# A searched instruction order, a last output tile in three pieces, and one weight's loads moved to the GpSimd queue

## The chip, the cores and the metric

One core of a Trainium2 chip. The metric is the device time of one execution in microseconds. The profile's span starts and ends a little inside the timed execution (266.0 us for a timed 267.67), so differences are taken within one kind of number only.

## The reference, cut to what matters

A gated mix of two branches over x of 2048 x 512: attention in four segments of 512 rows with 32 heads of 16 and a memory carried from segment to segment, and a gated linear unit of width 1792.

```python
g = sigmoid((x * gate_w).sum(-1, keepdims=True))
# attention: q, k, v = x@wq, x@wk, x@wv; per segment softmax(q k' + mask) v,
#   mixed with phi(q) M / (phi(q) z); then M += phi(k)' v, z += sum phi(k); o @ wo
# unit: h = relu(x @ W_gate) * (x @ W_up); h @ W_down
return g * a + (1 - g) * b
```

## The kernel before

The kernel is written as about a thousand small operations with names, engines, planned durations and keys. A planner, run when the kernel is built, orders them per engine, and that order is what is emitted. An array mode is the way in which TensorE's array is divided for a matmul: whole ("D"), row strips ("R"), strips of 64 x 32 ("P") or column strips ("C"). `f12.3` is the score block 3 of segment 1, head group 2; `pv12` its product with V; `mz0`, `den1` memory product and denominators; `g`, `u`, `d` the dense products of the unit, `q`, `k`, `v`, `wo` those of the attention, in operations of two matmuls.

```python
# the planner: TensorE takes the ready operation with the least key; a change of array mode is penalised
k = o.key
if o.mode == "P":            # product with V, 64 x 32 strips
    k += -20.0 if mode == "R" else 4.0
elif o.mode == "D" and mode == "C" and "C" not in o.flex:
    k += 3.0
...
o.ran = mode if mode in o.flex else o.mode   # dense work may stay in column strips ("C")

def mm(out_ap, lhsT, rhs, start, stop):
    if tiling[0] == "C":
        for j in range(4):                   # four column strips, four small matmuls
            q = slice(32 * j, 32 * j + 32)
            nc.tensor.matmul(out_ap[q], lhsT=lhsT[:, q], rhs=rhs, start=start, stop=stop, tile_position=(0, 32 * j))
    else:
        nc.tensor.matmul(out_ap, lhsT=lhsT, rhs=rhs, start=start, stop=stop)
...
def c_dummy(e):                              # "warm-up" matmuls on constants while x is loaded
    for _ in range(31):
        nc.tensor.matmul(g_dummy.t[:, 0:P], lhsT=ones, rhs=ones, start=True, stop=True)
...
x0_part(0, 0, "SP", -300)
x0_part(0, 1, "ACT", -300)
wq_part(0, 1, "ACT", -299)
x0_part(1, 0, "SP", -299)
x0_part(1, 1, "POOL", -110)
wq_part(1, 2, "SP", -298)
wq_part(2, 3, "POOL", -80)
wq_part(3, 4, "POOL", -79)
...
# wk's load waits for a one-element write into wk_sb, which waits for the first copied piece of x
o_wk0 = op("wk0", {"DVE": 0.08}, lambda e: nc.vector.memset(wk_sb[0:1, 0, 0:1], 0.0), key=-600, cls=0)
lw["wk"].deps.append((o_wk0, None))
```

## Time and profile before

| before | value |
|---|---|
| time, median of 3 runs | 267.61 us (267.2 to 268.28) |
| span of the profiled run | 265.97 us |
| busy: TensorE, ScalarE, VectorE, GpSimd | 98, 74, 68, 66% |
| first wk matmul to start of the last matmul | 10.23 to 262.30 us |
| instruction packets of queue 8, taken for TensorE's (why: under the load of x) | 21 of 16 KB |

TensorE is nearly always busy, so the table's third and fourth rows are the ones to read: the time is a head (before the first wk matmul), a stretch of TensorE work, and a tail. The lines that carry this are in the prediction.

### The profile page before, as it was taken

The numbers are of one execution on the slowest core, as the hardware profiler recorded it, in microseconds if no ns is written. First come the engines' busy times: TensorE is split into PE (matmuls) and PEld (weight loads), VectorE is DVE, ScalarE is ACT, GpSimd is POOL, SyncE is SP. The second block draws the span as 40 slices with busy tenths as digits, with TensorE's granted clock in tenths as the row PEclk, the third lists the DMA queues.
The fourth block names the chain that finished last, engine by engine and source line by source line (L and its number), as shares of the span: only waits on it lengthen the run. The fifth ranks groups of instructions, "written<-read, shape, count | busy, mean of one in ns | idle before, by whom it ended". The sixth has DMA issues, their size and how long they took to land.

```text
span 266.0 us, 6927 instructions
## 1 busy us (share of the span) xinstructions
PE 261.4 (98%) x2760; PEld 115.1 (43%) x2760; DVE 181.3 (68%) x408; ACT 195.7 (74%) x191; POOL 175.7 (66%) x436
## 2 busy tenths in 40 slices
PE   8999999999999999999999999999999999999994
PEld 7443344444344444444344434344434444344453
DVE  1496878998877188887988726678986625566611
ACT  3598899898976658999986668898788665876020
POOL 8338788884567678884567978886758876537000
PEclk9999999999999999999999999999999999999999
DMA  6898932224650100000582010000030010000011
GB/s 161 268 275 183 328 88 81 83 79 102 157 115 22 41 22 2 0 2 20 99 168 48 23 39 22 1 2 2 0 94 0 2 41 23 20 2 0 2 39 39
DMA packets 27728, 17.95 MB, mean 67 GB/s; under 512 B 13776, under 2 KB 27088, under 8 KB 27696
## 3 DMA queue, kind: packets, MB, share of 16 engines
q1 hardware_dynamic: 27136, 16.86, 24.8%
q0 software_dynamic: 144, 0.39, 0.6%
q8 instruction: 21, 0.34, 0.5%
q10 hardware_dynamic: 416, 0.26, 0.3%
q14 instruction: 11, 0.09, 0.1%
HBM read 9.84 MB, written 2.10 MB: 45 GB/s over the span
## 4 chain that ended last, share of the span: by engine, by line
PE 96%; DMA 2%; DVE 0%; issue 0%; DVEq 0%
PE G L248 78%; PE S L760 9%; PE G L872 7%; DMA wk_sb<-in_A_wk_dram 2%; PE G L290 1%; PE G L632 1%; PE G L809 0%; PE G L246 0%; PE G L406 0%; DVE os L721 0%; DVEq L721 0%
## 5 line engine op out<-in xcount | busy, mean ns | idle before, releaser
L774 ACT ACTIVATE E<-S 128x2048 bf16<-128x2048 f32 x72 | 135.1, 1876 | 31.9 <-PE S L760 25.7
L784 POOL TENSOR_SCALAR_AFFINE_SELECT E<-E 64x256 bf16<-64x256 bf16 x256 | 116.7, 456 | 54.4 <-ACT E L774 41.0
L248 PE MATMUL G<-xT,wu_sb 128*128 128x512 bf16 x224 | 59.8, 380 | 0.0
L248 PE MATMUL G<-xT,wg_sb 128*128 128x512 bf16 x224 | 59.3, 380 | 0.0
L248 PE MATMUL G<-wd_sb,hT 128*128 128x512 bf16 (+1 forms) x234 | 53.9, 367 | 0.0
L684 DVE TENSOR_TENSOR hT<-G,os 128x512 bf16<-128x512 f32 x56 | 38.2, 684 | 18.8 <-ACT os L680 9.4
L907 DVE STREAM_TRANSPOSE T<-G 128x512 f32<-128x512 f32 x44 | 30.4, 705 | 19.5 <-PE G L872 11.9
L680 ACT ACTIVATE os<-G 128x512 bf16<-128x512 f32 x56 | 32.8, 596 | 5.5 <-PE G L248 4.5
L248 PEld LDWEIGHTS <-hT 128*128 128x128 bf16 x234 | 21.4, 98 | 23.7 <-issue 2.8
L248 PEld LDWEIGHTS <-wu_sb 128*128 128x128 bf16 x224 | 20.2, 98 | 25.5 <-issue 3.9
L248 PEld LDWEIGHTS <-wg_sb 128*128 128x128 bf16 x224 | 20.2, 98 | 25.4 <-issue 3.7
L760 PE MATMUL S<-QT,K 32*128 32x192 bf16 (+7 forms) x512 | 28.6, 287 | 0.0
L760 PEld LDWEIGHTS <-K 32*128 32x128 bf16 x512 | 8.2, 92 | 29.9 <-issue 29.4
L872 PE MATMUL G<-E,Vp 64*32 64x128 bf16 (+7 forms) x512 | 18.8, 284 | 0.0
L872 PE MATMUL G<-E,VS 64*32 64x128 bf16 (+7 forms) x512 | 18.4, 284 | 0.0
L248 PE MATMUL G<-wo_sb,oT 128*128 128x512 bf16 (+1 forms) x68 | 18.0, 368 | 0.0
L721 DVE TENSOR_SCALAR os<-G,ngcol 128x512 bf16<-128x512 f32 (+1 forms) x10 | 6.9, 693 | 16.1 <-PE G L248 16.1
L248 PE MATMUL G<-xT,wk_sb 128*128 128x512 bf16 x64 | 16.5, 380 | 0.3 <-DMA wk_sb<-in_A_wk_dram 0.3
L723 ACT ACTIVATE os<-G,ngcol 128x512 bf16<-128x512 f32 x7 | 4.8, 687 | 16.1 <-PE G L248 16.1
L503 POOL COPY R<-rcol 32x4 f32<-32x4 f32 x64 | 14.1, 221 | 3.2
L949 POOL TENSOR_TENSOR O<-O,O 128x512 bf16<-128x512 bf16 x11 | 13.0, 1186 | 4.8 <-DVE O L927 4.1
L872 PEld LDWEIGHTS <-Vp 64*32 64x32 bf16 x512 | 12.2, 91 | 7.5 <-issue 4.2
(91 smaller groups left out, 278.1 us busy)
## 6 DMA issues: line engine op xcount, KB each, us to landing
VS<-Vp SPq DMA_DIRECT2D x8, 296.0 KB, 3.8
out_dram<-os SPq DMA_DIRECT2D x15, 128.0 KB, 1.7
xn<-in_A_x_dram SPq DMA_DIRECT2D x3, 512.0 KB, 4.3
wd_sb<-in_B_W_down_dram SPq DMA_DIRECT2D x3, 512.0 KB, 3.8
wg_sb<-in_B_W_gate_dram SPq DMA_DIRECT2D x2, 512.0 KB, 5.9
wu_sb<-in_B_W_up_dram SPq DMA_DIRECT2D x2, 512.0 KB, 6.4
wg_sb<-in_B_W_gate_dram SPq DMA_DIRECT2D x3, 256.0 KB, 7.2
wu_sb<-in_B_W_up_dram SPq DMA_DIRECT2D x3, 256.0 KB, 6.9
```

The costliest lines, as they stand in the source:

```text
L248: nc.tensor.matmul(out_ap, lhsT=lhsT, rhs=rhs, start=start, stop=stop)
L503: nc.gpsimd.tensor_copy(R[s][32 * j:32 * j + 32, k, :], rcol[32 * k:32 * k + 32, cols])
L680: nc.scalar.activation(rg.t[:], g.t[:], ACT.Relu)
L684: nc.vector.tensor_tensor(h.t[:], u.t[:], rg.t[:], ALU.mult)
L721: nc.vector.tensor_scalar(ob.t[:, cs], g.t[:, 0:W], ngcol[:, tt:tt + 1], None, ALU.mult)
L723: nc.scalar.activation(ob.t[:, cs], g.t[:, 0:W], ACT.Copy, scale=ngcol[:, tt:tt + 1])
L760: nc.tensor.matmul(sp.t[:, j, off:off + w], lhsT=K2[s, cc].t[rows, kb, :, :].rearrange("p r k -> p (r k)"), rhs=QT[s, cc].t[rows, L - w:L] ...
L774: nc.scalar.activation(eb_.t[:], sp.t[:], ACT.Exp, scale=SCALE)
L784: nc.gpsimd.affine_select(out=v, in_=v, compare_op=ALU.is_ge, fill=0.0, base=0, pattern=[[0, 4], [1, 64]], channel_multiplier=-1)
L872: nc.tensor.matmul(gs[r].t[32 * j:32 * j + 32, L - w:L], lhsT=v, rhs=src.t[rows, j, off:off + w], start=(kb == 0), stop=(kb == 7), tile_po ...
L907: nc.vector.transpose(T.t[:].rearrange("p b e -> p (b e)"), g.t[:])
L949: (nc.vector if e == "DVE" else nc.gpsimd).tensor_tensor(Oa.t[:], Oa.t[:], Ob.t[:], ALU.add)
```

## The change

Intent: fewer changes of array mode, at the same work, by shifting 85 planner keys found in a search; a shorter last scaling and store; and a Sync queue free of wq before wk.

```diff
+NUDGE = {
+    "d130.0": 50, "q21/0": 52, "k12/0": 45, "g0.10/0": 129, ... "xtr01": -12, ... "g0.2/1": 3,    # 85 in all, cut
+}
-    wq_part(1, 2, "SP", -298)
-    wq_part(2, 3, "POOL", -80)
-    wq_part(3, 4, "POOL", -79)
+    wq_part(1, 2, "POOL", -95)
+    wq_part(2, 4, "POOL", -80)
-        halves = 2 if tt == NT - 1 else 1
-        W = D // halves
-        for hf in range(halves):
+        for hf, (c0, W) in enumerate([(0, 256), (256, 128), (384, 128)] if tt == NT - 1 else [(0, D)]):
...            # W and the column slice passed on accordingly
+    for o in sc.ops:
+        o.key += NUDGE.get(o.name, 0)
     order = sc.run()
```

## The prediction

The sum: -0.95 + 0.05 - 0.17 + 0.2 + 0.1 = -0.77 us, and 267.61 - 0.77 = 266.84. Read from the profile of before: 0.106 us a change of mode, 0.45 us for two dense matmuls in column strips, 0.216 us a full matmul, and about 0.056 us a matmul of 128 columns (four in 0.22). That the four strips of a score block run side by side is seen at 14.22 us, where their matmuls start within 0.01 us; the 0.22 us for them is the estimate from the 0.216. Two terms are estimates: 0.05 us for the 32 KB store, from 1.5 us for 64 KB and 1.7 for 128 KB, and 0.2 us for wk, as it was not shown that the GpSimd queue's loads hold it up.

> **What bounds the kernel now.** I read the busy shares first, then the chain of work that ended last, then the waits of TensorE, then single stretches of its timeline.
>
> ```profile
> PE 261.4 (98%) x2760; PEld 115.1 (43%) x2760; DVE 181.3 (68%) x408; ACT 195.7 (74%) x191; POOL 175.7 (66%) x436
> ...
> PE 96%; DMA 2%; DVE 0%; issue 0%; DVEq 0%
> ```
>
> TensorE is busy nearly all the span and carries 96% of the chain. No other engine is above 74%. A busy PE is not a PE at its peak, so the question is what its 261 us consist of. The waits of TensorE alone are two lines:
>
> ```profile
> PE G L290 <- PEq L1032: 0.8, 1, 0.8
> PE G L248 <- DMA wk_sb<-in_A_wk_dram: 0.3, 1, 0.3
> ```
>
> So from 10.23 us, when wk has landed, to the last matmul at 262.6 us there is no wait at all. No reordering can remove waits there; it can only make the same matmuls pass faster. The chain in order of time shows what is lost between them:
>
> ```profile
> 4.89 5.29 DMA wk_sb<-in_A_wk_dram
> 10.18 0.05 issue
> 10.23 4.06 PE G L248 x18
> 14.28 0.33 PE S L760 x4
> 14.61 2.70 PE G L248 x12
> ...
> 32.87 0.33 PE S L760 x8
> 33.20 1.10 PE G L872 x64
> 34.30 0.97 PE G L248 x4
> ...
> 241.35 5.72 PE G L248 x26
> ```
>
> L248 are full-array matmuls of 512 columns, L760 the attention scores in four row strips of the array, L872 the product with V in strips of 64 by 32. Runs of 26 and of 12 full matmuls take 5.72 and 2.70 us: 3.02 us for 14 more, 0.216 us each. Then 12 would take 2.59, and the run took 0.11 more; four would take 0.86 and took 0.97. Every run thus pays about 0.106 us once, at its beginning. The score block fits this too: 0.33 us, where four strips of 512 columns running side by side need about 0.22. It is the price of a change between ways of dividing the array, the same whichever kind follows: the V product takes 1.10 us after a score block (33.20) and also after full matmuls (61.65).
>
> I counted these changes in the instruction order of the kernel before, from the first wk matmul on: 173 (68 full to score, 65 back, 16 V product to full, 9 full to V product, 7 score to V product, 4 into and 4 out of column strips). 173 x 0.106 = 18.3 us, 7% of the run. The rest is 894 full matmuls x 0.216 = 193.0, 36 of 256 columns in the last tile x 0.109 = 3.9 (14 of them take 1.53 us between 258.47 and 260.00), and 36.8 for scores, V products, memory products and denominators. The sum is 252.1 us; the trace has 262.58 - 10.23 = 252.35. The units are good to 0.3 us.
>
> [...] The trace has two column-strip dense pairs already, and it costs little there: eight strip matmuls (two dense ones) take 0.45 us instead of 0.43. [...] four 128-column transposes pass in 0.22 us at 6.68 us. [...]
>
> **The change, part by part.**
>
> *The order.* The 85 shifts only move planner keys, so the set of matmuls stays the same except in the last tile. The built order of the changed kernel has 161 changes instead of 173. Score blocks followed directly by a V product go from 7 to 14, and one V product is followed directly by a score block; each such meeting saves one change. The four column-strip blocks (denominators, memory products) now follow a score block directly (4 of 4, before 0 of 4). Gain: 12 x 0.106 = 1.27 us, all of it on the path, as TensorE never waits. But the planner lets dense work stay in column strips once there: 20 dense pairs instead of 2. Each costs 0.45 - 0.43 = 0.018 us more: 18 x 0.018 = 0.32 us lost. Net gain 0.95.
>
> *The last tile.* Two pieces of 256 columns become one of 256 and two of 128. Eighteen matmuls of 256 columns (1.97 us) become 36 of 128 columns at 0.056 (2.02 us): 0.05 lost. After the last matmul there remain the scaling on VectorE and one store:
>
> ```profile
> 262.68 0.48 DVE L721 TENSOR_SCALAR os<-G,ngcol 128x256 bf16<-128x256 f32 x1 [1.55 <-PE G L248]
> 263.19 0.33 SPq L729 DMA_DIRECT2D out_dram<-os  x1
> ```
>
> The scaling takes 0.48 us for 256 columns and about 0.72 for 512, so 0.12 per 128 columns: 0.36 for the new last piece, 0.12 gained. The store lands after 1.5 us for 64 KB and 1.7 for 128 KB; for 32 KB I estimate 0.05 less[...]. Tail gain 0.17.
>
> *The head.* Here TensorE does wait, 0.35 us for wk. Its load is held back by a small VectorE write into wk_sb, placed behind the first copy of x:
>
> ```profile
> 4.55 0.29 DVE L414 COPY xT<-G 128x256 bf16<-128x256 bf16 x1 [3.17 <-PE G L406]
> 4.76 0.38 ACT L416 ACTIVATE xT<-G 128x256 bf16<-128x256 bf16 x1 [1.40 <-PE G L406]
> 4.78 0.06 DVE L351 MEMSET wk_sb<- 1x1 bf16 x1
> 4.89 0.37 SPq L347 DMA_DIRECT2D wk_sb<-in_A_wk_dram  x1
> 4.94 0.42 PE L428 MATMUL S<-const-bfloat16-1.0 128*128 128x128 bf16 x2
> 4.98 0.29 DVE L414 COPY xT<-G 128x256 bf16<-128x256 bf16 x1
> ```
>
> The new order swaps the first two pairs of transposes and puts that write behind VectorE's second copy. A pair of transposes takes 0.21 us here, so the first VectorE copy moves to about 4.76, the second to about 5.05, and the write to about 5.27: wk is issued 0.48 us later, at about 5.37. Against this, the part of wq that stood ahead of wk in the Sync queue is gone. The packet records show 1024-byte packets in that queue from 4.5 to about 6.5 us, the amount of that part, and wk's packets only then, at a low rate until about 7.3 us, while the GpSimd queue moves its large packets (4.2 to 6.8 us). With first packets 1.1 to 1.4 us after issue, as the last store and the first x load show, a wk issued at 4.89 could have started at 6.0 to 6.3 but was held to about 6.5. Issued at 5.37 it starts at 6.5 to 6.8. So most of the delay is paid back. But 128 KB more must go through the GpSimd queue[...]. I take a landing 0.2 us later: 0.2 lost. The wq parts themselves should be in time: part 1, issued at about 2.8 us, is needed at 6.9 (its neighbours took 3.8); parts 2 and 3 together, issued at about 3.4, are needed at 8.0.
>
> *New small waits* on TensorE: an allowance of 0.1 us, as an order packed closer can hardly wait less than nothing.
>
> Sum: -0.95 + 0.05 - 0.17 + 0.2 + 0.1 = -0.77 us; 267.61 - 0.77 = 266.84.
>
> **The rivals.** First, **waits take the place of the changes saved**. Moving a V product next to a score block moves its operands' deadline. I summed TensorE work in the order between the last score block a V product needs and the product itself: least 6.1 us in the new order, 5.8 in the old. What must fit in is one exponential (1.88 us) and at most four masks (4 x 0.456 us), 3.7 us plus hand-overs, so slack stays near 2 us. Starts of neighbouring score blocks are at least 2.6 us apart (2.4 in the old), against 1.88 for the exponential that frees the score buffer. The planner was also told that GpSimd work is longer than it is: a masking pair is entered at 1.007 us with its 6% surcharge, and two masks take 0.91. This speaks against the rival. But reordering on VectorE and ScalarE touches hundreds of hand-overs that I did not sum; if a handful of waits of 0.2 us appear, the time is 267.6 to 268.
>
> Second, **the head decides**: if the later issue of wk counts in full, the head costs 0.5 and the kernel takes 267.1; if freeing the Sync queue makes wk land before the last wq matmul ends (9.88 us), 0.35 is gained instead and it takes 266.3. The packet times favour the middle.
>
> Third, **column-strip dense runs cost more than the two samples show**, since four to six pairs stand in a row now, each matmul with four weight loads. At 0.05 us a pair the loss is 1.0 us in place of 0.32 and the time is 267.5. Against it: the eight weight loads of the sample passed in 0.15 us, far ahead of their matmuls.
>
> **Range and chances.** Everything removable is a small share of the 18.3 us of changes, and everything that could be lost is a small wait or two, so 2% (5.4 us) is out of reach in either direction unless some engine falls far behind. The three runs of before spread over 1.1 us, which alone is larger than my gain. I predict 266.8 us, 266.1 to 267.8; within 2% 0.97, faster 0.015, slower 0.015.
>
> **What would show it right or wrong.** Right: the chain still over 95% TensorE; score blocks of 0.33 us followed at once by 1.10 us of V product about fourteen times; from the first wk matmul to the last matmul about 251.4 us (252.35 - 0.95 + 0.05); column-strip dense pairs at 0.45 us; the last scaling near 0.36 us; wk issued near 5.4 and landing near 10.4. Wrong: TensorE lines that wait for ScalarE, VectorE or GpSimd inside the stretch; the first wk matmul before 10.0 or after 10.8; column-strip pairs above 0.47; the 128-column matmuls of the last tile at 0.08 us instead of 0.056.

## More of the kernel before

One row of the page is added here, as it turned out to matter; its columns are queue and kind, packets, MB, and share of the 16 DMA engines' time:

```profile
q8 instruction: 21, 0.34, 0.5%
```

## The result, and the profile after

| | before | after |
|---|---|---|
| time, median of 6 runs each | 267.79 us (267.2 to 268.28) | 266.81 us (266.6 to 267.19) |
| first wk matmul | 10.23 | 9.42 us |
| stretch: that to the start of the last matmul | 252.07 | 252.25 us |
| tail: start of the last matmul to the end | 3.68 | 3.34 us |
| span | 265.97 | 265.01 us |

The ratio is 0.9967, 95% interval 0.9953 to 0.9982. Ratios here are the mean time of one kernel's fast runs over that of the other's of the same rounds, so not quite the ratio of the medians quoted.

The predicted 266.8 us came true, but not from the terms it was made of: in these two profiles the head gains 0.81, the tail 0.34, and the stretch, where nearly all the gain should lie, loses 0.18. The waits of TensorE after (columns: who waited, on whom, us in total, times, longest):

```profile
PE G L264 <- issue: 1.7, 11, 0.2
PE G L886 <- issue: 1.1, 1, 1.1
PE G L306 <- PEq L1048: 0.8, 1, 0.8
```

The eleven waits of 0.2 us are not real. The page counts fewer matmul records than there are weight loads and instructions:

```profile
PE 256.7 (97%) x2853; PEld 116.7 (44%) x2886; DVE 183.6 (69%) x413; ACT 193.4 (73%) x187; POOL 175.2 (66%) x436
```

The program has 2886 matmuls; 33 records are missing, and each leaves a hole. For the same reason the chain's 92% TensorE and its pieces of ScalarE are not to be read as new limits: between two score blocks the time is still that of the matmuls in the order. In the second profile of the changed kernel no record is missing, and its chain is 96% TensorE. The one wait of 1.1 us is real, as its weight loads are all there and stand still too. The chain in order of time around it (start, us, what; L647 the memory product, L262 column strips, L774 scores, L886 product with V):

```profile
31.09 0.64 PE G L647 x64
31.73 1.75 PE G L262 x32
33.48 0.33 PE S L774 x8
33.81 1.06 PE G L886 x51
34.87 1.14 issue
36.00 0.27 PE G L886 x8
```

The stop is in the middle of one V product, between two of its matmuls, and "issue" says that the profile shows no semaphore it waited for. In the kernel before the same product took 1.10 us in one piece; here it takes 1.06 + 1.14 + 0.27 = 2.47, so the stop costs 1.37 us and not only its idle 1.14.

Head and tail after, from the timeline (start, us, engine, what):

```profile
5.21 0.06 DVE L366 MEMSET wk_sb<- 1x1 bf16 x1
5.32 0.37 SPq L362 DMA_DIRECT2D wk_sb<-in_A_wk_dram  x1
9.42 2.33 PE L264 MATMUL G<-xT,wk_sb 128*128 128x512 bf16 x10
...
260.72 0.94 PE L264 MATMUL G<-wd_sb,hT 128*128 128x128 bf16 x14
261.50 0.39 PE L264 MATMUL G<-wo_sb,oT 128*128 128x128 bf16 x4
261.93 0.35 DVE L735 TENSOR_SCALAR os<-G,ngcol 128x128 bf16<-128x128 f32 x1 [0.58 <-PE G L264]
```

wk is issued late, at 5.32 us as predicted, but is there at 9.37 and not at 10.4. The 128-column matmuls pass at (261.50 - 260.72) / 14 = 0.056 us, and the last scaling takes 0.35: both as predicted.

### The profile page after: what moved, and what is told of

It is laid out like the page before. It is cut to its first block, busy times and chain, and to the rows that moved or that the text cites. A ratio compares the mean times of both kernels' runs of the same rounds, so it can differ in the third digit from the quotient of the medians.

```text
span 265.0 us, 7147 instructions
## 1 busy us (share of the span) xinstructions
PE 256.7 (97%) x2853; PEld 116.7 (44%) x2886; DVE 183.6 (69%) x413; ACT 193.4 (73%) x187; POOL 175.2 (66%) x436
## 4 chain that ended last, share of the span: by engine, by line
PE 92%; issue 3%; ACT 2%; DMA 2%; DVE 0%; ACTq 0%
PE G L264 71%; PE S L774 9%; PE G L886 7%; PE G L262 3%; DMA wk_sb<-in_A_wk_dram 2%; PE G L306 1%; PE G L647 1%; ACT E L788 1%; ACT Vp L556 0%; PE G L823 0%; ACT QT L556 0%; ACT etq L579 0%; DVE xT L429 0%; ACT os L695 0%; PE G L421 0%
## 5 line engine op out<-in xcount | busy, mean ns | idle before, releaser
L264 PE MATMUL G<-xT,wg_sb 128*128 128x512 bf16 x200 | 53.9, 380 | 0.6 <-issue 0.3
L264 PE MATMUL G<-wd_sb,hT 128*128 128x512 bf16 (+2 forms) x239 | 53.1, 354 | 1.4 <-issue 1.1
L264 PE MATMUL G<-xT,wu_sb 128*128 128x512 bf16 x196 | 53.0, 380 | 0.2
L264 PEld LDWEIGHTS <-hT 128*128 128x128 bf16 x252 | 22.2, 98 | 24.0 <-issue 2.4
L264 PEld LDWEIGHTS <-wg_sb 128*128 128x128 bf16 x208 | 18.9, 98 | 23.2 <-issue 2.5
L264 PEld LDWEIGHTS <-wu_sb 128*128 128x128 bf16 x202 | 18.7, 98 | 23.3 <-issue 2.8
L774 PE MATMUL S<-QT,K 32*128 32x192 bf16 (+7 forms) x512 | 28.6, 287 | 0.3
L735 DVE TENSOR_SCALAR os<-G,ngcol 128x512 bf16<-128x512 f32 (+2 forms) x13 | 8.7, 669 | 19.5 <-PE G L264 19.4
L774 PEld LDWEIGHTS <-K 32*128 32x128 bf16 x512 | 8.2, 92 | 30.2 <-issue 30.1
L886 PE MATMUL G<-E,Vp 64*32 64x128 bf16 (+7 forms) x512 | 19.0, 284 | 1.1 <-issue 1.1
L886 PE MATMUL G<-E,VS 64*32 64x128 bf16 (+7 forms) x512 | 18.5, 284 | 0.0
L264 PE MATMUL G<-wo_sb,oT 128*128 128x512 bf16 (+2 forms) x71 | 16.9, 355 | 0.2 <-issue 0.2
L886 PEld LDWEIGHTS <-Vp 64*32 64x32 bf16 x512 | 12.2, 91 | 7.3 <-issue 4.9
L941 DVE TENSOR_TENSOR O<-T,sm 128x256 bf16<-128x256 f32 x32 | 14.9, 498 | 0.2
L264 PE MATMUL G<-wv_sb,xT 128*128 128x512 bf16 x62 | 14.9, 380 | 0.1
```

Of the source, the lines that this page charges most:

```text
L735: nc.vector.tensor_scalar(ob.t[:, cs], g.t[:, 0:W], ngcol[:, tt:tt + 1], None, ALU.mult)
L774: nc.tensor.matmul(sp.t[:, j, off:off + w], lhsT=K2[s, cc].t[rows, kb, :, :].rearrange("p r k -> p (r k)"), rhs=QT[s, cc].t[rows, L - w:L] ...
L886: nc.tensor.matmul(gs[r].t[32 * j:32 * j + 32, L - w:L], lhsT=v, rhs=src.t[rows, j, off:off + w], start=(kb == 0), stop=(kb == 7), tile_po ...
L941: nc.vector.tensor_tensor(O.t[:, :, r, :], T.t[:, :, 0:DH], sm.t[:, r, :, None].to_broadcast([P, 16, DH]), ALU.mult)
```

## The experiments

Theory after the first reading: the stretch did gain what was predicted, and a stop in the supply of TensorE's instructions takes it back. Rivals stand with each run. All results were correct. By size each run is "same" (within 2%); what is told apart is told by the intervals. "Before" in a ratio is the kernel before on the same chip in the same rounds.

### The changed kernel again

No edit.

> The changed kernel once more, unaltered. Theory (instruction supply): the stop of 1.1 us inside the first V product (34.9 to 36.0 us in the first profile) comes from the order of instructions and the loads running beside it, so it comes back, 0.8 to 1.4 us long at about the same place; the first wk matmul starts at 9.4 us if the TensorE clock is at full rate by 5.2 us, at about 9.9 if it is still slow at 6 us as in the kernel before. Rival (chance): the stop was one profile's accident; then it is absent here and the span is about 264.0. Either way 0.8 to 1.0 us faster than before in the timed runs.

Measured: 266.71 us, ratio 0.9971 (0.9953 to 0.9989). The stop is there again, 0.90 us, at 34.70 us, before the same matmul: the 350th weight load of the program has not started when 349 have, in this profile and in the first. So it is no accident. The "clock" of this and later expectations is the spacing of 128-column matmuls, 0.107 us early in a run and 0.056 later: the change came at about 3.9 us here, 5.2 in the first profile of the changed kernel and 6.4 in that of before.

### The order alone

```diff
 # wq queues and the two halves of the last tile as before; NUDGE applied
```

> The 85 shifts alone: the wq queues and the two halves of the last tile as before. Theory: 12 changes of mode saved and 18 column-strip pairs more give 0.95 us, the stop inside the first V product takes 1.1 back, and wk, issued 0.4 us later behind a part of wq in the same queue, lands about 0.2 to 0.4 later: 0.3 to 0.5 us slower than before, 268.1. Rival (the prediction on record, no stop): 0.95 gained less 0.2 to 0.5 in the head: 0.5 to 0.7 us faster, 267.1.

Measured: 266.79 us, ratio 0.9977 (0.9958 to 0.9995), about 0.6 us faster. The stop was there, 0.82 us, so the rival was wrong in having none; but the theory was wrong in the sum. It had compared with the first profile of before. The runs below show that most profiles of before have an earlier head and a stop of their own.

### The head alone

```diff
-    wq_part(1, 2, "SP", -298)
-    wq_part(2, 3, "POOL", -80)
-    wq_part(3, 4, "POOL", -79)
+    wq_part(1, 2, "POOL", -95)
+    wq_part(2, 4, "POOL", -80)
```

> Only the two wq lines: wq part 1 in the GpSimd queue and parts 2 and 3 as one load; order and last tile as before. Theory (queue order): wk is issued at 4.9 us as before but no wq part stands ahead of it, so it takes about 4.1 us instead of 5.3 and lands near 9.0; TensorE then waits for nothing and the first wk matmul follows the last wq matmul at 9.35 (clock early at full rate) or 9.95 (late): 0.3 to 0.9 us faster than before. Rival (the prediction: more bytes in the GpSimd queue hold wk up): landing 10.0 to 10.3, 0 to 0.2 us faster.

Measured: 267.27 us, ratio 0.9995 (0.9976 to 1.0014): no gain to be seen, a miss for the theory. wk landed at 9.03, as the theory had it, and the first wk matmul started at 9.43. But the stretch grew to 252.68 us. The chain shows why, at 138 us (L484 is the gate's product on x of segment 2, L906 a transpose that frees a buffer of G, the PSUM bank that a later matmul writes):

```profile
129.44 6.40 DMA xn<-in_A_x_dram
...
135.87 0.70 DVE xn L484 x2
136.56 0.54 DVE T L906
137.10 0.02 issue
137.12 0.71 DVE xn L484 x2
137.83 0.64 DVE T L906
138.47 0.04 issue
138.51 1.02 PE G L248 x4
```

The load of x lands at 135.84 us. Two VectorE products wait for it with the transposes of PSUM banks standing behind them in the order, and TensorE waits for a bank: its matmuls start at 138.51 us, 0.04 after the second transpose ends. This gives back about 0.6 us (252.68 - 252.07). In the first profile of before, which came late out of its head, TensorE issues its matmuls across 138 us without a wait.

### The tail alone

```diff
 # the three pieces of the last tile; keys not shifted, wq queues as before
```

> Only the last output tile in three pieces (256, 128, 128); order and wq queues as before. Both theories: 36 matmuls of 128 columns at 0.056 us instead of 18 of 256 (0.05 us more), last scaling 0.35 instead of 0.48, store about the same: 0.1 us faster, within noise. If the 128-column matmuls took 0.08 us each, 0.7 us slower.

Measured: 267.39 us, ratio 0.9996 (0.9977 to 1.0016), unclear as expected. In its profile the tail is 3.26 us, against 3.68 or 3.69 in all five profiles with two halves (before three times, order alone, head alone); with three pieces it is 3.33 to 3.35 in the eight others. That is 0.34 less, of which 0.05 is only that the last matmul is shorter.

### The kernel before, a second and a third time

No edit.

> The kernel before once more, for a second profile of its head and its stream. Theory: the wait for wk is a property of the queues, so wk lands between 9.6 and 10.2 us, later than TensorE's last wq matmul (9.3 to 9.9, by when the clock reaches full rate), and there is no stop over 0.5 us in the stream. Rival: the head of before is bound by the clock just like the head of the changed kernel, and the 10.18 us of the first profile was a slow outlier: then wk lands before 9.5.

> The kernel before a third time, one look, for its head and for the wait at 138 us. Theory: wk lands at 9.5 to 10.2 us; where TensorE starts on it before 9.7 us, the stop of about 0.5 us at 138 us (VectorE held by the x load of segment 2) appears, where it starts later than 10 us it does not. Rival: the stop at 138 us comes and goes without regard to the head.

Measured, one look each: 267.58 and 267.28 us; spans 265.88 and 265.57. wk landed at 9.54 and 9.22 us, so the 10.18 of the first profile was a late one, and the theory's lower limit of 9.5 was too high. Both stretches are long (252.61 and 252.62) and both have the wait at 138 us. Over the five profiles with the old order, TensorE starts on wk at 9.26, 9.43, 9.58, 9.69 (tail alone) and 10.23; the first three have the stop at 138 us, the last two do not. That fits the theory, but the head is not all of it. In the three with the stop the load of x took 6.2 to 6.4 us and landed at 135.57 to 135.84; in the two without it took 5.2 and landed at 135.65 and, in the tail alone, at 135.06. There TensorE was only 0.11 us later than in the profile of 9.58, and the load 0.6 us earlier. What counts is the load against TensorE; why it takes 5.2 or 6.3 us stays open. In the nine profiles with the new order it lands at 131.3 to 134.7 and nothing waits for it.

### The load of x for segment 1 behind five weight loads

```diff
     order = sc.run()
+    at = {o.name: i for i, o in enumerate(order)}
...            # a check of the places, cut
+    order.insert(at["wo"], order.pop(at["xn1"]))
```

> The changed kernel with one Sync-queue load moved: the load of x for segment 1 (which waits until VectorE has read the old x, about 31 us) goes behind the five weight loads that stood behind it, so these 2 MB go at about 25 to 29 us, as in the kernel before, and not at 31 to 36. Compute order unchanged. Theory (instruction supply slowed by loads): the instruction fetch near 33 us is no longer beside them, the stop of 0.8 to 1.1 us in the first V product goes or shrinks below 0.3, and the kernel is 0.7 to 1.1 us faster than the changed one: about 265.8. Rival (the stop is the burst of small matmuls itself, whatever the loads): unchanged, 266.7, stop still 0.8 or more.

Measured: 270.62 us, ratio 1.0120 (1.0098 to 1.0142), slower instead of faster. The stop did not go; it became 2.91 us, at the same matmul:

```profile
33.87 1.06 PE G L886 x51
34.92 2.91 issue
37.84 0.27 PE G L886 x8
```

My theory had the wrong moment. I had read the fetch at 33 us as the moment of asking. The trace's packet records of queue 8 beside TensorE's weight loads give another reading. Queue 8 is taken for TensorE's, as its packets go with the matmuls: 21 for 2760, 22 for 2886, 23 for the 2926 of a later run, while the other instruction queue has 11 in every profile. They are of 16 KB, and from the first to the last TensorE starts 2579 weight loads in 20 packets in the first profile of before and 2688 in 21 in that of the changed kernel, 128 to 129 a packet. So I count one block for each 128 matmul pairs (a weight load and a matmul each, 256 instructions). As the stop stands after pair 349, the block limits should lie near pairs 93, 221, 349, 477 and so on, and, as I read the table below, what is asked for near pair 221 is needed at pair 350. The moment of asking is not recorded. As a mark for it the table takes the weight load six or seven pairs ahead of the limit; at some later limits a packet starts up to 2.2 us before this mark, so the lags are rough (us; "stop" is idle time):

```
                     mark at 221  packet starts  lag   packet ends  mark at 349  stop
before                   33.15        34.44      1.29     35.52        40.98     none
before, second           32.50        33.14      0.64     34.08        40.34     none
before, third            32.19        34.46      2.27     35.55        40.03     none
after                    31.14        33.09      1.96     34.49      stops 34.87  1.14
after again              30.97        33.33      2.35     34.30      stops 34.70  0.90
order alone              31.21        33.28      2.08     34.47      stops 34.95  0.82
x load last              31.19        35.25      4.06     36.39      stops 34.92  2.91
```

In all four stops TensorE resumes 1.3 to 1.5 us after the packet's end. What differs between the orders is the time to the next limit. Memory product, strips, scores and V product stand together in the new one, 64 + 32 + 8 + 64 small matmuls in 4 us, so 128 pairs pass in 3.3 us and not in 7.8. The old order could afford a lag of 2.27 us; the new one cannot.

What the loads do to the lag is not shown. Five weight loads and x, 3 MB, are issued from 30.9 us on in the new order, because the order of VectorE holds the x load until then. In the kernel before they are issued at 24.6 to 29 us but still land until 34 to 36, so its fetch runs beside more traffic (248 to 270 GB/s during the lag, in its three profiles) than that of the changed kernel (133 and 160), and its lag is mostly shorter. In the experiment the traffic is 330 GB/s and the lag 4.06, but the head alone has 322 GB/s and a lag of 1.44. So the theory missed, and what made this fetch so late stays open.

The other five timed runs of the experiment took 270.4 to 271.6 us, 1.9 to 3.0 us more than the profiled one (268.56), at a granted clock of 0.986 to 0.994 against 1.000. The ratio therefore mixes the stop with a lower clock, whose cause is open; the stop itself costs 4.24 - 1.10 = 3.14 us, and the stretch, 254.04 us, is otherwise that of the changed kernel.

### Strips written as full-array matmuls

```diff
-            tiling[0] = o.ran
+            tiling[0] = o.mode if o.mode == "D" else o.ran
```

> The changed kernel with the 20 dense pairs that stayed in column strips written as full-array matmuls at the same places: 120 fewer small matmuls, 4 more changes of mode. Theory (instruction supply): the burst before the first V product has 24 fewer small matmuls of about 136, so the stop there shrinks by some 0.3 to 0.6 us; 4 x 0.106 more and 20 x 0.018 less: 0.1 slower elsewhere; in sum 0.2 to 0.5 us faster than the changed kernel, about 266.4. Rival (the fetch is late because of the loads alone): stop unchanged, 0 to 0.1 us slower than the changed kernel.

Measured: 266.06 us, ratio 0.9939 (0.9921 to 0.9958): faster than the changed kernel by more than expected. The stop is gone entirely:

```profile
33.64 0.33 PE S L774 x8
33.97 1.10 PE G L886 x64
35.07 1.40 PE G L264 x6
```

The mark at 349 is now reached at 35.45 us, after the V product and not inside it, with the packet's end at 34.03. This counts against loads alone as the cause: they were the same, and the lag was 1.59 us, or 1.98 in the run with strips and swap both out, which has no stop either. The edit also adds six changes of mode, not four (167 in the trace, for 161); an estimate of 6 x 0.106 = 0.64 us for them fits the stretch, 251.44 us here and 250.89 in the next run but one.

### Without the swap of the first transposes

```diff
-    ... "pr11.1": -8, ... "xtr01": -12,
+    ... "pr11.1": -8, ...
```

> The changed kernel without the shift that swaps the first two pairs of transposes, so that the VectorE write that releases wk stands behind the first copy again and wk is issued at 4.9 instead of 5.3 us. Theory: wk lands near 9.0 and no longer bounds; TensorE starts on it when the last wq matmul is through, 9.0 to 9.95 by the clock: 0 to 0.4 us faster than the changed kernel, by run. Rival: wk's landing is set by what the DMA engines carry and stays at 9.2 to 9.4: same time.

Measured: 266.58 us, ratio 0.9957 (0.9941 to 0.9974), the changed kernel's time within the noise. wk was issued at 4.89 and landed at 9.30 us, no earlier than the 9.21 to 9.37 of the two profiles of the changed kernel. So the later issue costs nothing that these runs can show. The stop was there, 1.15 us, and ended 1.5 us after the packet's end.

### Forty pairs more ahead of all work

```diff
-        for _ in range(31):
-            nc.tensor.matmul(g_dummy.t[:, 0:P], lhsT=ones, rhs=ones, start=True, stop=True)
+        for _ in range(71):
+            nc.tensor.matmul(g_dummy.t[:, 0:56], lhsT=ones, rhs=ones[:, 0:56], start=True, stop=True)
```

> The changed kernel with 71 warm-up matmuls of 56 columns in place of 31 of 128: nearly the same columns, 40 more matmul pairs ahead of all work. All work, its order and the loads stay. TensorE instructions come in blocks of 16 KB, 128 pairs; in the changed kernel two block limits lie 3.3 us apart around the memory product, the strips and the first V product (31.1 and 34.5 us), and the block asked for at the first limit is usable only about 4.9 us later. Shifted by 40 pairs, these limits fall at about 27 and 33 us or later, over 5 us apart. Theory (a block limit inside the burst, with its fetch held up by loads): the stop of 0.9 to 1.1 us in the first V product is gone, and the time is 0.7 to 1.1 us below the changed kernel, 265.8, unless the warm-up itself grows by some tenths. Rival (the stop belongs to the V product itself, a late mask or a bank): stop unchanged, 266.7.

Measured: 265.59 us, ratio 0.9927 (0.9911 to 0.9944), the fastest kernel here. After the warm-up, work, order and loads are those of the changed kernel; the block limits moved. The mark at 221 is now passed at 27.78 us, the packet starts 0.60 us later and ends at 29.56, the next mark is crossed at 34.27, and the V product is whole again:

```profile
34.00 0.33 PE S L774 x8
34.33 1.10 PE G L886 x64
```

The stretch is 250.89 us although wk came late in this profile (9.89). A late mask or a bank of the V product would not have gone away.

### Strips and swap both out

```diff
 # the edits of the strips and of the swap together
```

> Both trims that helped or did not hurt: the changed kernel with the 20 dense pairs as full-array matmuls and without the shift that swaps the first transposes. Theory: no stop in the first V product, wk issued at 4.9 us and landing near 9.2, head bound by the clock or by wk in turn: 0 to 0.2 us faster than with the strips alone taken out: 265.9 to 266.1. Rival: the earlier head is given back by another wait: same as with the strips alone taken out or up to 0.3 slower.

Measured: 265.96 us, ratio 0.9944 (0.9923 to 0.9964); first wk matmul at 9.52, stretch 251.44, no stop. The same as with the strips alone out; the two trims do not add.

### Twenty pairs more

```diff
-        for _ in range(31):
-            nc.tensor.matmul(g_dummy.t[:, 0:P], lhsT=ones, rhs=ones, start=True, stop=True)
+        for _ in range(51):
+            nc.tensor.matmul(g_dummy.t[:, 0:78], lhsT=ones, rhs=ones[:, 0:78], start=True, stop=True)
```

> As the shift by 40 pairs, but by 20: 51 warm-up matmuls of 78 columns. Theory (block limits): the stop does not go but moves with the limit. In the changed kernel it stands before the 349th matmul pair, inside the first V product, 0.9 to 1.1 us long; with 20 more pairs ahead it stands again before about the 349th pair of the program, which is now 20 pairs earlier in the work, still inside the V product or just before it, at 34.2 instead of 34.6 us, and is a few tenths longer (1.1 to 1.5 us), as the limits are closer. Time 266.7 to 267.1. Rival (any change of the warm-up frees the stop, or it belongs to a particular matmul): no stop, 265.6, or a stop at the same matmul as before.

Measured: 265.74 us, ratio 0.9938 (0.9917 to 0.9958). A miss for the theory's size, and half of one for its place. There is a pause before pair 350, 20 pairs earlier in the work as expected, but it is only 0.13 us: the V product takes 1.23 and not 1.10.

```profile
33.51 0.33 PE S L774 x8
33.84 1.23 PE G L886 x62
35.07 1.40 PE G L264 x6
```

The limits were 2.97 us apart, closer than in the changed kernel, but this time the packet started 0.98 us after the mark (31.05 us), not 2, and ended at 32.95. The x load was issued 0.12 us before the mark here and 0.24 before it in the first profile of the changed kernel. That the request slipped in ahead of the loads' packets is a guess that no run shows. The Sync queue's issues after x differ too: the second took 1.45 us for 0.52 there, the fourth 0.51 for 1.85. No run separates these, and it stays open. What holds is the end of the fetch: TensorE resumes at 34.48 us, 1.5 us after it, as in the five longer stops (1.3 to 1.5), and in the eight profiles without a stop pair 350 comes at least 1.87 us after the packet's end. The lag alone does not give the length: 1.96 us went with a stop of 1.14 and 2.35 with one of 0.90.

## Why the prediction was right

**Bound and unit costs: right.** TensorE stayed the bound. The weight loads of the traces show 173 changes of mode before and 161 after, and 14 score blocks followed at once by a V product, as counted.

**Changes saved: right.** The stretch should have come to 252.07 - 0.90 = 251.17 us. Without what the stop costs, the changed kernel has 252.25 - 1.37 = 250.88 and 252.02 - 1.13 = 250.89, and the run with shifted limits, which has no stop, 250.89. The tail alone, with the same last tile and no stop at 138 us, has 252.16: twelve changes less are worth 1.27 us, 0.106 each, with the strips in it.

**Column strips: mis-sized, on the safe side.** Blocks of 32, 40 and 48 strip matmuls took 1.75, 2.17 and 2.59 us, which is 0.432 to 0.438 us a pair, not 0.45, against 0.432 for a full pair. The loss is at most 18 x 0.006 = 0.1 us, not 0.32. The third rival, that longer runs of strips cost more, was wrong as to their own time. But the strips' extra instructions are what put the block limit inside the V product.

**Last tile: right in kind, low by 0.1 to 0.2.** Matmuls at 0.056 and scaling of 0.35 us are as predicted. The last store lands 1.48 us after its issue and 1.56 before, so it gains 0.08 and not 0.05; yet the tail shortened by 0.34 and not by 0.17. The rest, 0.12, lies between the starts of the last matmul and of the scaling (0.26 us, before 0.38), 0.05 of it the shorter matmul.

**Head: wrong in sign, small in effect.** I predicted wk 0.2 us later on the strength of one profile in which it was late, for a reason that no run shows. The two profiles of the changed kernel have it at 9.21 and 9.37, the three of before at 9.22, 9.54 and 10.18. The spread is larger than any gain, and the head alone gained nothing in time. The packet times in the prediction's head were also read 0.31 us too late: I took a wrong zero for them. The delays of 1.1 to 1.4 us that they are compared with have the same error (0.83 and 1.11 with the right zero), so that comparison stands.

**New waits: the step that failed.** The allowance was 0.1 us, and the first rival looked for late operands. What came was a stop for want of instructions, idle 0.8 to 1.15 us and costing 1.0 to 1.4, which no sum over operands shows. It takes back about the whole gain in the stretch, 1.18 us (252.07 - 250.89). From the first wk matmul to the end of the last matmul it was 252.47 us and not 251.4, and the first wk matmul came at 9.42, before 10.0: by the prediction's own list both speak against it. The stop went unnoticed in the total because the old order had a loss that I had not seen either: about 0.5 to 0.6 us are given back at 138 us, in three of five profiles. None of the profiles with the new order waits there. So the new order trades a frequent half microsecond at 138 us and about 1.2 us of mode changes for a stop that costs 1.0 to 1.4 us at 35 us, and the tail adds 0.3. That the sum was 266.8 is largely luck; the range was honest, the terms were not all.

**The parts add up** in the timed runs: 0.23% for the order, 0.05 for the head, 0.04 for the tail, 0.32 in all, and 0.33 for the whole change; each is known to about 0.2, so the two small ones are not told from zero and the fit proves little.

## What to carry to other kernels

When the bounding engine is full, count what it pays between its pieces (here 0.106 us at each of 173 changes of mode), and check a gain against several profiles of the old kernel, as one may hold a loss or a late load that others do not. Small instructions cost supply as well as time here: with the bursts of small matmuls packed together, 128 pairs in 3.3 us, TensorE stood still for 0.8 to 1.15 us in four profiles, and forty harmless pairs ahead of all work took the stop away, for 0.4%. Look at an "issue" wait in the middle of an operation with that in mind.
